# Weight blocks for the later slots fetched a turn ahead, in halves, with the cast behind the item's own

## The chip, the core and the metric

The kernel runs on one core of a Trainium2 chip. A core has five engines that run their own instruction rows in order and wait for each other by semaphores: TensorE (PE in the profile; PEld is its weight load), VectorE (DVE), ScalarE (ACT), GpSimd (POOL) and SyncE (SP), which here issues nearly all DMAs. The metric is the time of one execution on the device, in microseconds, as the median of several runs. One further execution is profiled; its own time is given beside the median.

## What is computed

A two-dimensional Fourier transform of x [8, 3072, 256] (real part), seen as 24576 tokens of 256 numbers, then a layer of 8 experts of which each token uses one, then a plain layer with a squared ReLU:

```python
X = np.fft.fft(np.fft.fft(x, axis=1), axis=2).real.astype(np.float32)
x = X.reshape(8 * 3072, 256)
e_idx = np.argmax(x @ w_gate, axis=1)            # the expert of a token
for e in range(8):
    mask = e_idx == e
    h = np.maximum(x[mask] @ w1[e], 0.0)         # w1[e] is 256 x 1024
    out[mask] = gate_w[mask, None] * eom[mask, e, None] * (h @ w2[e])   # w2[e] is 1024 x 256
h = np.maximum(out @ w_in, 0.0)                  # w_in is 256 x 2048
return (h * h) @ w_out                           # w_out is 2048 x 256
```

`gate_w` and `eom` are a softmax weight and a sigmoid of `x @ w_output_gate`. All is float32.

## The kernel before

A float32 matmul is made of three products of a rounded high part and a remainder: h is x cast to the type that PE reads (fp32r), l is x - h, and the product takes hh, hl and lh. So every operand is *split*: ACT casts, and DVE or POOL subtracts. In the names of the profile xh/xl, hh/hl, zh/zl, wih/wil and woh/wol are such pairs.

**Fourier part.** Eight batches go through `fft` and `group` (lines 148 to 343). DVE adds and multiplies along the first axis (tile X, lines 158 and 161), PE multiplies by tables loaded as trig (L258, SP) into pz, ACT casts zh (L273), DVE makes zl (L274), PE makes pd from them (L281). Tokens are sorted by expert and scattered by POOL into a DRAM array xs (L340), in groups of six scatters.

**Expert part.** Tokens are taken from xs in slots of 256, all of one expert (tile xr, L556). A slot has 12 items. Four a-items (`items_a`) do the expert layer: first matmuls into ph, then ACT casts hh (L682) and DVE makes hl (L683), then second matmuls into py. Eight c-items (`items_c`) do the last layer for the slot before: matmuls into ph, three ACT instructions (L853 rl, L854 square, L857 hh) and one of DVE (L858 hl) in `squares`, then matmuls into po, whose result goes out by POOL (L740). `push` gives the order: an item's first matmuls, its evacuation, and then the second matmuls of the item three before.

**Weights of a slot.** The first 40 slots ("single") hold the raw weights of their expert in two tiles r1 and r2 (`expert`, SP, L603 and L604), and split them on the way: ACT casts w (L615), POOL subtracts (L616). The later slots ("paired") read weights that were split beforehand from a DRAM array wq (L582, SP). `presplit` fills wq: for each of 64 blocks it fetches raw values (SP, L595), casts them into the first half of a tile cut (ACT, L596), subtracts into the second half (POOL, L597) and writes cut to wq (SP, L598). Raw and cut have one room each. It is a generator; `build` draws one block from it at every sixth item, from item 66 on.

**What sets the order.** `build` runs the items and draws from the Fourier generator at a set pace between them. The instruction order on each engine is then set by a scheduler that goes by data dependencies, rooms and program order; an instruction without an edge to the item next to which it was written can be moved far ahead. `issue_after(x)` puts the instructions in its block behind instruction x on their engine's row. In the order of before, the casts of presplit stand beside items 0 to 132 of 472 in the single stage.

Of the kernel before, what the change touches and what calls it, by code (L numbers as in the profile page):

```python
# [10 lines left out]
F32 = mybir.dt.float32  # L11
F32R = mybir.dt.float32r
# [3 lines left out]
AF = mybir.ActivationFunctionType  # L16
ALU = mybir.AluOpType
# [4 lines left out]
P = 128  # L22
S = 3072
D = 256
E = 8
# [74 lines left out]
class Kern:  # L100
# [485 lines left out]
    def presplit(self):  # L586

        nc = self.nc
        for e in range(E):
            for k in range(4):  # L590
                for j, src in enumerate((self.a["w1"][e].rearrange("(c p) f -> p c f", p=P)[:, :, k * 256:k * 256 + 256],
                                         self.a["w2"][e].rearrange("(c p) f -> p c f", p=P)[:, 2 * k:2 * k + 2])):
                    r = self.fp.tile([P, 2, 256], F32, name="raw")
                    o = self.fp.tile([P, 2, 2, 256], F32R, name="cut")
                    nc.sync.dma_start(out=r, in_=src)  # L595
                    nc.scalar.copy(out=o[:, 0], in_=r)  # L596
                    nc.gpsimd.tensor_tensor(out=o[:, 1], in0=r, in1=o[:, 0].bitcast(F32), op=ALU.subtract)  # L597
                    nc.sync.dma_start(out=self.wq[e, k, :, j * 1024:j * 1024 + 1024], in_=o.rearrange("p t c f -> p (t c f)").bitcast(F32))  # L598
                    yield

    def expert(self, q, w1, w2, **kw):
        flat = lambda w: w.rearrange("o (c p) f -> p (o c) f", p=P)
# [70 lines left out]
    def items_a(self, sl):  # L673
        st = {}
        for i in range(4):
            def mm1(i=i):
                st[i] = self.first(self.w[:, i, 0], self.w[:, i, 1], sl["x"], 0)

            def evac(i=i):
                h = self.ap.tile([P, 512], F32R, name="hh", bufs=4)  # L680
                l = self.ap.tile([P, 512], F32R, name="hl", bufs=4)
                self.nc.scalar.activation(out=h, in_=st[i], func=AF.Relu)  # L682
                self.evac = self.nc.vector.scalar_tensor_tensor(out=l, in0=st[i], scalar=0.0, in1=h.bitcast(F32), op0=ALU.max, op1=ALU.subtract)  # L683
                st[i] = (h, l)

            def mm2(i=i):
                if i == 0:
                    st["y"] = self.ps.tile([P, 512], F32, name="py", tag="y", bufs=1)
                h, l = st[i]
                for c in range(2):  # L690
                    k = slice(c * 256, c * 256 + 256)
                    for dc in range(2):
                        d = slice(dc * P, dc * P + P)
                        wh, wl = self.w[:, i, 2, c, d], self.w[:, i, 3, c, d]
                        self.products(st["y"][:, dc * 256:dc * 256 + 256], [(wh, h[:, k]), (wh, l[:, k]), (wl, h[:, k])],
                                      i == 0 and c == 0 and dc == 0, i == 3 and c == 1 and dc == 1)
                if i == 3:
                    if self.strassen:
                        ys = self.yp.tile([P, 2, SLOT], F32, name="ys", tag="yl" if sl["tail"] or self.both and sl["i"] % 2 else "yh", bufs=2)
                        self.nc.scalar.copy(out=ys, in_=st["y"].rearrange("p (c t) -> p c t", c=2))  # L700
                        if sl["tail"]:
                            self.nc.sync.dma_start(out=self.yt[:, :, bass.ds(sl["col"], SLOT)], in_=ys)
                        sl["y"] = ys
                    else:
                        sl["y"] = self.split(st["y"], self.yp, "y", 2)

            yield mm1, evac, mm2

    def items_c(self, sl):
# [140 lines left out]
    def squares(self, ps):  # L850

        r = self.yp.tile([P, 512], F32, name="rl", bufs=2)
        self.nc.scalar.activation(out=r, in_=ps, func=AF.Relu)  # L853
        self.nc.scalar.activation(out=ps, in_=r, func=AF.Square)  # L854
        h = self.ap.tile([P, 512], F32R, name="hh", bufs=4)
        l = self.ap.tile([P, 512], F32R, name="hl", bufs=4)
        self.nc.scalar.copy(out=h, in_=ps)  # L857
        self.evac = self.nc.vector.tensor_tensor(out=l, in0=ps, in1=h.bitcast(F32), op=ALU.subtract)  # L858
        return h, l

# [226 lines left out]
@with_exitstack  # L1087
def build(ctx, tc, a, B, plan, pace=1.25):

    kk = Kern(tc, a, B)  # L1090
    kk.n_tail = B * S // SLOT - sum(n for _, n in plan)
    nt = kk.n_tail + E - 1
    right = ctx.enter_context(ExitStack())
    left = ctx.enter_context(ExitStack())
    pool = lambda name, **kw: left.enter_context(tc.tile_pool(name=name, bufs=1, **kw))
    cp, wp, ps, dp = pool("cp"), pool("wp"), pool("ps", space=PSUM), pool("dp", space=DRAM)
    kk.ap = kk.tp = pool("ap")
    fp = right.enter_context(tc.tile_pool(name="fp", bufs=1, side="right"))
    kk.snaps = {nb: cp.tile([1, E], F32, name=f"snap{nb}") for nb, _ in plan}
    done = 0  # L1100

    def all_ffts():
        nonlocal done
        while done < B:
            yield from kk.fft(done)
            done += 1

    kk.fp = fp
    ffts = all_ffts()
    next(ffts)  # L1110
    with tc.tile_pool(name="st0", bufs=1) as st:
        kk.setup(cp, fp, st, ps, dp)
    kk.moe_setup(wp)

    def ffts_to(nb):
        while done < nb:
            next(ffts, None)

    tables = {}
    cut = kk.presplit()  # L1120

    def opener(w):
        def open_(u):
            nb, n = plan[w]
            if w not in tables:
                ffts_to(nb)
                with tc.high_priority():
                    if w < len(plan) - 1:
                        tab, ex = kk.table(n, kk.snaps[nb])
                        tables[w] = tab, kk.changes(ex), None  # L1130
                    else:
                        for _ in cut:
                            pass
                        right.close()
                        kk.tp = tp = right.enter_context(tc.tile_pool(name="tp", bufs=1, side="right", reuse_waits="tile"))
                        tab, ex = kk.table(n, kk.snaps[nb])
                        tab2, ex2 = kk.table(nt, kk.snaps[nb], tail=True)
                        tables[w] = tab, kk.changes(ex, ex2[:, 0:KEEP]), tab2
                        kk.zero_tails()
            tab, chg, tab2 = tables[w]  # L1140
            u["tab"] = tab2 if u["tail"] else tab
            u["chg"] = chg[:, u["i"]:u["i"] + 1]
        return open_

    units = []
    for w, (nb, n) in enumerate(plan):
        kinds = [False] * n
        if w == len(plan) - 1:
            kinds = [False, True, False] * KEEP + [False] * (n - 2 * KEEP)
        c = [0, 0]  # L1150
        for i, tail in enumerate(kinds):
            units.append(dict(i=i, j=c[tail], tail=tail, w=w, batches=nb, paired=w == len(plan) - 1, open=opener(w)))
            c[tail] += 1
    g = kk.run(units)
    ffts_to(plan[0][0])
    kk.yp = pool("yp")
    kk.early, kk.due, kk.rate = 12, 0.0, 1.25
    kk.other = (1, 2)
    kk.second = kk.second_weights()
    for _ in range(8):  # L1160
        next(g)

    acc, at = 0.0, 8
    ends = np.cumsum([12 * n for _, n in plan])
    for _ in g:
        at += 1
        if at > ends[0] and at % 6 == 0 and at < ends[2]:
            next(cut, None)
        w = int(np.searchsorted(ends, at, side="right"))
        if w + 1 < len(plan):  # L1170
            acc += pace * FFT_COST * (plan[w + 1][0] - plan[w][0]) / (12 * plan[w][1] - (8 if w == 0 else 0))
            while acc > 0:
                with tc.issue_after(kk.evac.ins) if at > ends[0] else ExitStack():
                    c, wait = next(ffts, (1e9, True))
                acc -= c
                if wait:
                    break
# [24 lines left out]
```

## Time and profile before

| quantity | value |
|---|---|
| median of 3 runs | 3777.5 us (3771.97 to 3778.32) |
| the profiled execution | 3795.63 us |
| its span in the trace | 3793.8 us |
| PE busy | 3578.2 us, 94% of the span |
| ACT, DVE, POOL busy | 57%, 56%, 28% |
| mean granted clock of PE | 0.981 of full speed |

The span is the profiled execution as its engines show it; the execution's own time is 1.8 us longer, and 18.1 us longer than the median. Single stage: to about 1767 us. The busy share is a mean over stages: below, the page's 40 slices (94.8 us each) show where it is lower, and tables by stretch give it in microseconds. "a <- b" in a list of waits reads: a stood still until b had come. L12 is a line of the kernel before.

### The profile page before, as it was taken

Reading aid. Unit: us, or ns where it says so; the run is one execution under the profiler, and the core shown is the slowest. Engines: PE = TensorE matmul, PEld = TensorE weight load, DVE = VectorE, ACT = ScalarE, POOL = GpSimd, SP = SyncE. Lnnn points to the kernel's source line nnn. Section 1 sums busy time; section 2 is a strip of 40 time slices with the busy share of each in tenths; the row PEclk is TensorE's granted clock in tenths of the full one; section 3 lists DMA queues with packets and bytes.
Section 4 is the critical chain, followed back from the end, with each engine's and each line's share of the span. In section 5 each row is a group of like instructions: output and inputs, shape, how many; then the busy total and the mean of one; then the engine's idle time right before and its main releaser. Section 6 shows DMA issues by size and latency. Waiting matters only on the chain. (4 is left out here: it accounts for less than half of the span.)

```text
span 3793.8 us, 76990 instructions
## 1 busy us (share of the span) xinstructions
PE 3578.2 (94%) x29484; PEld 3521.6 (93%) x29484; DVE 2118.2 (56%) x4043; ACT 2174.7 (57%) x4377; POOL 1047.9 (28%) x1196
## 2 busy tenths in 40 slices
PE   4578988999999999999999999999999999999998
PEld 4577888999999999999999999999899999999997
DVE  7975555576767576325344445444455555555554
ACT  3455555656666566666355555555566666656665
POOL 4765565445454455432000000000000000000000
PEclk8799999999999999999999999999999999999999
DMA  6445454322222211012234343443210100101000
GB/s 204 158 140 175 146 184 165 129 75 93 67 86 74 94 65 61 30 37 85 87 133 152 131 171 137 141 147 132 88 67 18 60 26 24 51 21 51 27 15 12
DMA packets 172851, 356.40 MB, mean 94 GB/s; under 512 B 21824, under 2 KB 125504, under 8 KB 157120
## 3 DMA queue, kind: packets, MB, share of 16 engines
q1 hardware_dynamic: 152960, 296.49, 23.4%
q0 software_dynamic: 19520, 54.94, 3.9%
q8 instruction: 235, 3.85, 0.4%
q14 instruction: 136, 1.11, 0.1%
HBM read 431.40 MB, written 89.85 MB: 137 GB/s over the span
## 5 line engine op out<-in xcount | busy, mean ns | idle before, releaser
L651 PE MATMUL po<-woh,hh 128*128 128x256 f32 x3072 | 861.7, 281 | 8.2 <-ACT hh L857 8.0
L651 PE MATMUL po<-wol,hh 128*128 128x256 f32 x3072 | 860.4, 281 | 3.0 <-POOL wol L414 3.0
L651 PE MATMUL po<-woh,hl 128*128 128x256 f32 x3072 | 859.5, 281 | 1.3 <-DVE hl L858 0.6
L651 PE MATMUL ph<-xh,w 128*128 128x256 f32 x3200 | 651.7, 285 | 27.9 <-DVE hl L683 15.4
L651 PE MATMUL py<-hh,w 128*128 128x256 f32 x3200 | 635.5, 282 | 1.0 <-ACT hh L682 0.6
L651 PEld LDWEIGHTS po<-woh,hh 128*128 128x128 f32 x3072 | 581.5, 189 | 12.4 <-ACT hh L857 11.9
L651 PEld LDWEIGHTS po<-wol,hh 128*128 128x128 f32 x3072 | 580.3, 189 | 3.4 <-POOL wol L414 3.4
L651 PEld LDWEIGHTS po<-woh,hl 128*128 128x128 f32 x3072 | 578.6, 189 | 5.2 <-DVE hl L858 4.5
L651 PEld LDWEIGHTS ph<-xh,w 128*128 128x128 f32 x3200 | 527.8, 191 | 29.4 <-DVE hl L683 15.8
L683 DVE SCALAR_TENSOR_TENSOR hl<-ph,hh 128x512 fp32r<-128x512 f32 x400 | 275.3, 689 | 481.9 <-ACT hh L682 466.2
L651 PEld LDWEIGHTS py<-hh,w 128*128 128x128 f32 x3200 | 519.8, 189 | 5.4 <-ACT hh L682 3.4
L682 ACT ACTIVATE hh<-ph 128x512 fp32r<-128x512 f32 x400 | 238.6, 597 | 483.0 <-PE ph L651 459.7
L616 POOL TENSOR_TENSOR w<-r,w 128x512 fp32r<-128x512 f32 x320 | 426.3, 1346 | 269.7 <-ACT w L615 268.3
L651 PE MATMUL ph<-xl,w 128*128 128x256 f32 x1600 | 456.1, 285 | 1.0 <-DVE xl L623 1.0
L651 PE MATMUL py<-hl,w 128*128 128x256 f32 x1600 | 453.4, 283 | 0.7 <-DVE hl L683 0.7
L858 DVE TENSOR_TENSOR hl<-ph,hh 128x512 fp32r<-128x512 f32 x320 | 220.0, 688 | 405.6 <-ACT hh L857 384.5
L740 POOL DMA_INDIRECT out<-ot,id x192 | 196.6, 1024 | 785.8 <-DVE ot L739 748.7
L651 PE MATMUL ph<-yh,wih 128*128 128x256 f32 x1280 | 372.7, 291 | 35.6 <-DVE hl L858 31.2
L645 POOL CAST id<-xr 128x2 uint32<-128x2 f32 x88 | 20.4, 232 | 1292.9 <-DMA xr<-xs 1286.1
L651 PE MATMUL ph<-yl,wih 128*128 128x256 f32 x1280 | 361.4, 282 | 1.0 <-issue 1.0
L651 PE MATMUL ph<-yh,wil 128*128 128x256 f32 x1280 | 361.6, 283 | 0.0
L858 DVE TENSOR_TENSOR hl<-px,hh 128x512 fp32r<-128x512 f32 x224 | 154.8, 691 | 325.2 <-ACT hh L857 323.5
(279 smaller groups left out, 8406.6 us busy)
## 6 DMA issues: line engine op xcount, KB each, us to landing
w<-wq SPq DMA_DIRECT2D x240, 1024.0 KB
r<-w SPq DMA_DIRECT2D x78, 1024.0 KB
wq<-cut SPq DMA_DIRECT2D x64, 512.0 KB
xr<-xs SPq DMA_DIRECT2D x100, 260.0 KB
raw<-w SPq DMA_DIRECT2D x64, 256.0 KB
trig<-c_trig SPq DMA_DIRECT2D x104, 128.0 KB
X<-x SPq DMA_DIRECT2D x8, 1024.0 KB
X<-x SPq DMA_DIRECT2D x8, 768.0 KB
```

The source lines that it names most:

```text
L616: nc.gpsimd.tensor_tensor(out=l, in0=r, in1=h.bitcast(F32), op=ALU.subtract)
L645: self.nc.gpsimd.tensor_copy(out=i, in_=ids)
L651: self.nc.tensor.matmul(out=out, lhsT=l, rhs=r, start=first and i == 0, stop=last and i == len(pairs) - 1, skip_group_check=True)
L682: self.nc.scalar.activation(out=h, in_=st[i], func=AF.Relu)
L683: self.evac = self.nc.vector.scalar_tensor_tensor(out=l, in0=st[i], scalar=0.0, in1=h.bitcast(F32), op0=ALU.max, op1=ALU.subtract)
L740: q = self.nc.gpsimd.indirect_dma_start(out=self.a["out"], out_offset=bass.IndirectOffsetOnAxis(ap=ids[:, t:t + 1], axis=0), in_=o[:, t, : ...
L858: self.evac = self.nc.vector.tensor_tensor(out=l, in0=ps, in1=h.bitcast(F32), op=ALU.subtract)
```

## The change

`presplit` works on 128 half units of [128, 256] instead of 64 blocks of [128, 512]. The raw tile has two rooms; the fetch for the next unit is given at the end of a unit's turn, the first one ahead of all. The tile cut is half as large and still has one room. The cast is placed, by `issue_after`, behind the last ACT instruction of the item that was written last (`self.cast`, L682 or L857 of before). `build` draws a unit at every third item, from item 75 on. In the changed file the lines of presplit are 594 (fetch), 602 (cast), 603 (subtract) and 605 (write); L615 becomes 623, L682 690, L853 to L858 become 861 to 866.

```diff
     def presplit(self):
 
         nc = self.nc
-        for e in range(E):
-            for k in range(4):
-                for j, src in enumerate((self.a["w1"][e].rearrange("(c p) f -> p c f", p=P)[:, :, k * 256:k * 256 + 256],
-                                         self.a["w2"][e].rearrange("(c p) f -> p c f", p=P)[:, 2 * k:2 * k + 2])):
-                    r = self.fp.tile([P, 2, 256], F32, name="raw")
-                    o = self.fp.tile([P, 2, 2, 256], F32R, name="cut")
-                    nc.sync.dma_start(out=r, in_=src)
-                    nc.scalar.copy(out=o[:, 0], in_=r)
-                    nc.gpsimd.tensor_tensor(out=o[:, 1], in0=r, in1=o[:, 0].bitcast(F32), op=ALU.subtract)
-                    nc.sync.dma_start(out=self.wq[e, k, :, j * 1024:j * 1024 + 1024], in_=o.rearrange("p t c f -> p (t c f)").bitcast(F32))
-                    yield
+        units = [(e, k, j, c) for e in range(E) for k in range(4) for j in range(2) for c in range(2)]
+
+        def fetch(e, k, j, c):
+            r = self.fp.tile([P, 256], F32, name="raw", bufs=2)
+            src = self.a["w2" if j else "w1"][e].rearrange("(c p) f -> p c f", p=P)
+            nc.sync.dma_start(out=r, in_=src[:, 2 * k + c] if j else src[:, c, k * 256:k * 256 + 256])
+            return r
+
+        r = fetch(*units[0])
+        yield
+        for (e, k, j, c), nxt in zip(units, units[1:] + [None]):
+            o = self.fp.tile([P, 2, 256], F32R, name="cut")
+            with self.tc.issue_after(self.cast.ins):
+                nc.scalar.copy(out=o[:, 0], in_=r)
+            nc.gpsimd.tensor_tensor(out=o[:, 1], in0=r, in1=o[:, 0].bitcast(F32), op=ALU.subtract)
+            to = self.wq[e, k, :, j * 1024:j * 1024 + 1024].rearrange("p (t c f) -> p t c f", t=2, c=2)
+            nc.sync.dma_start(out=to[:, :, c], in_=o.bitcast(F32))
+            r = nxt and fetch(*nxt)
+            yield
...
-                self.nc.scalar.activation(out=h, in_=st[i], func=AF.Relu)
+                self.cast = self.nc.scalar.activation(out=h, in_=st[i], func=AF.Relu)
...
-        self.nc.scalar.copy(out=h, in_=ps)
+        self.cast = self.nc.scalar.copy(out=h, in_=ps)
...
-        if at > ends[0] and at % 6 == 0 and at < ends[2]:
+        if at > ends[0] + 12 and at % 3 == 0 and at < ends[2]:
             next(cut, None)
```

ACT's row at the end of one slot's w casts, before. In the names, the number behind a tile is one use of it; r2_133 is the raw half of the expert's weights, py and ph are PE's results:

```order
L857 CAST hh_6073<-ph_6057 128x512
L622 CAST yh_6089<-py_5973 128x512
L615 CAST w_134<-r2_133 128x512
L596 CAST cut_18178<-raw_18177 128x512
L853 ACTIVATE rl_6111<-ph_6098 128x512
L854 ACTIVATE ph_6098<-rl_6111 128x512
```

The same place now:

```order
L865 CAST hh_6081<-ph_6065 128x512
L630 CAST yh_6097<-py_5975 128x512
L623 CAST w_134<-r2_133 128x512
L861 ACTIVATE rl_6119<-ph_6106 128x512
L862 ACTIVATE ph_6106<-rl_6119 128x512
L865 CAST hh_6122<-ph_6106 128x512
L602 CAST cut_6147<-raw_6025 128x256
```

The cast, ahead of the next item's evacuation before (L853 to L857), stands behind it now. Its block, number 18177 of the program before, was written for item 342 of the program; number 6025 was fetched beside this place.

SP's row around the same place, before:

```order
L598 DMA wq_135<-cut_17600 128x1024
L595 DMA raw_17834<-w2 128x2x256
...
L603 DMA r1_132<-w1 128x2x1024
L598 DMA wq_135<-cut_17835 128x1024
L595 DMA raw_18177<-w1 128x2x256
...
L604 DMA r2_133<-w2 128x8x256
```

And now:

```order
L605 DMA wq_135<-cut_6265 128x2x256
L594 DMA raw_6398<-w1 128x256
L605 DMA wq_135<-cut_6394 128x2x256
L594 DMA raw_6507<-w2 128x256
...
L611 DMA r1_132<-w1 128x2x1024
L605 DMA wq_135<-cut_6503 128x2x256
L594 DMA raw_6634<-w2 128x256
```

Before, a write of block n is followed by the fetch of block n + 1 (cut_17835 is made from raw_17834). Now the write of unit n is followed by the fetch of unit n + 2: cut_6394 is made from raw_6269, and raw_6398, fetched ahead of that write, becomes cut_6503.

## Rows read from the trace of the kernel before

**Rows 1.** The page's 40 slices (94.8 us each): busy tenths, and granted clock.

```profile
PE   4578988999999999999999999999999999999998
PEclk8799999999999999999999999999999999999999
```

**Rows 2.** By stretch: length, PE, PEld, DVE, ACT, POOL busy (instructions), clock, DMA share, GB/s.

```profile
220.00:700.00 480.00, 411.49 (x3231) 399.75 (x3230) 273.88 (x559) 263.15 (x546) 277.14 (x284) 0.94 0.50 165
700.00:1511.00 811.00, 794.14 (x6735) 786.05 (x6734) 539.22 (x1056) 500.56 (x1014) 405.89 (x449) 1.00 0.24 79
1511.00:1735.00 224.00, 222.93 (x1900) 222.89 (x1900) 71.06 (x124) 142.98 (x249) 83.32 (x80) 1.00 0.13 43
```

**Rows 3.** Waits, 220 to 705 us, ACT and PE: us in total, times, longest.

```profile
ACT cut L596 <- DMA raw<-w: 127.8, 46, 8.6
...
PE pd L281 <- ACT zh L273: 23.2, 15, 3.1
PE ph L651 <- DVE hl L858: 21.6, 12, 5.2
...
PE ph L651 <- DVE hl L683: 4.1, 2, 2.1
PE pt L631 <- DMA xr<-xs: 3.0, 1, 3.0
```

**Rows 4.** Waits, 705 to 1511 us, ACT and PE.

```profile
ACT rl L853 <- PE ph L651: 88.6, 105, 3.9
ACT w L615 <- PE ph L651: 87.1, 70, 2.0
...
PE ph L651 <- DVE hl L858: 5.1, 3, 2.6
PE pd L281 <- ACT zh L273: 4.4, 5, 1.3
```

**Rows 5.** In order of time, 300 to 312 us: start, length, instruction, [idle before].

```profile
303.38 0.43 SPq L595 DMA_DIRECT2D raw<-w  x1
...
307.18 0.62 ACT L596 CAST cut<-raw 128x512 fp32r<-128x512 f32 x1 [2.58 <-DMA raw<-w]
...
309.88 0.82 PE L281 MATMUL pd<-mh,zh 128*128 128x290 f32 x2 [3.05 <-ACT zh L273]
```

**Rows 6.** In order of time, 556 to 572 us, four engines.

```profile
563.12 0.38 SPq L595 DMA_DIRECT2D raw<-w  x1
...
567.23 0.62 ACT L596 CAST cut<-raw 128x512 fp32r<-128x512 f32 x1 [8.27 <-DMA raw<-w]
...
569.62 0.69 DVE L858 TENSOR_TENSOR hl<-ph,hh 128x512 fp32r<-128x512 f32 x1 [2.19 <-ACT hh L857]
...
570.37 0.58 PE L651 MATMUL ph<-yh,wih 128*128 128x256 f32 x1 [4.29 <-DVE hl L858]
```

**Rows 7.** By line: ns shortest/median/longest, first and last start in us, shapes.

```profile
L596 ACT CAST cut<-raw x64: 602/620/632, 32.3 to 694.6; 128x512 fp32r<-128x512 f32 x64
...
L597 POOL TENSOR_TENSOR cut<-raw,cut x64: 1261/1292/2251, 37.2 to 695.5; 128x512 fp32r<-128x512 f32 x64
...
L407 ACT CAST wih<-conv x16: 401/406/428, 66.2 to 140.7; 128x256 fp32r<-128x256 f32 x16
...
L413 POOL TENSOR_TENSOR conv<-conv,woh x16: 728/914/1717, 148.9 to 211.4; 128x256 f32<-128x256 f32 x16
...
L598 SPq DMA_DIRECT2D wq<-cut x64: 343/356/427, 38.5 to 696.8; - x64
...
L582 SPq DMA_DIRECT2D w<-wq x240: 73/220/370, 1783.1 to 3668.8; - x120
```

**Rows 8.** In order of time, ACT, 1635 to 1672 us: two a-items' w casts.

```profile
1665.94 0.62 ACT L615 CAST w<-r 128x512 fp32r<-128x512 f32 x1 [0.93 <-PE ph L651]
...
1668.79 0.62 ACT L615 CAST w<-r 128x512 fp32r<-128x512 f32 x1 [1.73 <-PE ph L651]
```

**Rows 9.** Groups by line, POOL, 705 to 1511 us: busy us, mean ns, idle before.

```profile
L340 POOL DMA_INDIRECT xs<-R,pi x108 | 118.5, 1097 | 79.3 <-DVE R L337 41.0 <-issue 25.7 <-ACT hh L857 5.2
```

## The prediction

> **What bounds the kernel now.** I read the slices of the page first, then the busy time by stretch, then the lists of waits, then two stalls in order of time. The slices show TensorE (PE) at nine tenths or more from the eighth slice on, and below that, at a lower granted clock, before it [rows 1]. So the first 700 us hold nearly all that is left to win. The stretches put a size on it [rows 2]. From 220 to 700 us PE is busy for 411.49 of 480 us and does 3231 matmuls, 6.73 a microsecond. From 700 to 1511 us the same mixture of Fourier work and expert items goes on, and PE does 6735 in 811 us, 8.30 a microsecond. At that pace the 3231 would take 3231 / 8.305 = 389 us, so the stretch holds **91 us** above what the next one shows to be possible. They are of two kinds. Idle time: 480 - 411.49 = 68.5 us, of which the later stretch's 16.9 us over 6735 matmuls (2.5 ns each) would leave 8; that is 60 us too much. Slow work: a matmul costs 411.49 / 3231 = 127.4 ns instead of 117.9, and 9.45 ns x 3231 = 30.5 us. The granted clock is 0.94 there and 1.00 later, and 6% of 411 us is 25 us. In the slices the clock is lowest where PE pauses most [rows 1], so a pause seems to cost more than its own length.
>
> What pauses it: in 220 to 705 us ScalarE (ACT) stands still for 127.8 us, 46 times, in front of the presplit's cast, because the raw block has not landed [rows 3]. PE does not read that cast's result at all. It waits for what stands behind it on ACT: for zh directly (23.2 us) and for hl, which VectorE makes from ACT's hh (21.6 and 4.1 us). In 705 to 1511 us, which holds no presplit cast (all 64 lie at 32.3 to 694.6 us, [rows 7]), the same waits are 4.4 and 5.1 us [rows 4]. Two stalls show the chain. At 303.38 us SP issues a raw fetch, the cast starts at 307.18 after 2.58 us of waiting, zh follows two instructions later, and PE has idled for 3.05 us at 309.88 [rows 5]. The second is worse: raw issued at 563.12, since one raw room forces it to wait for the subtract before it, cast at 567.23 after 8.27 us, hl at 569.62, PE at 570.37 after 4.29 us [rows 6]. The cast stands in ACT's row at a place where its data cannot yet be there.
>
> **The change part by part.** *Fetch one turn ahead, two rooms.* In the new order a write is followed by the fetch for the unit after the next, so a raw block is asked for two turns, six items, before its cast. An item in the calm stage takes 2.85 us (1665.94 to 1668.79, [rows 8]), so six are 17 us, against 3.8 us from issue to cast in [rows 5]. The wait of 127.8 us goes nearly whole. What PE gets of it: the lower bound is the waits that name the chain, 23.2 + 21.6 + 4.1 = 48.9 us, less what the later stretch would have of them (9.5 us x 485 / 806 = 5.7): 43 us. The upper bound is the 91. I take 43 + 25 of clock = **68 us**, because the low clock follows from the pauses, and leave the rest of the idle time (17 us) to VectorE's and the Fourier chain's own waits, which stay.
>
> *The cast placed behind the item's own, units half as large.* The casts leave ACT's first 500 us and spread over items 75 to about 460; the instructions that they now stand between ran at some 510 to 1735 us in the trace of before. Their number doubles. A cast of 128x512 takes 0.62 us, one of 128x256 0.406 [rows 7]: 64 x 0.62 = 39.7 us become 128 x 0.406 = 52.0 us. Where they come to, ACT is free for 811 - 500.56 = 310 us and 224 - 142.98 = 81 us [rows 2], and it waits for PE there, 88.6 and 87.1 us [rows 4], up to 1.73 us before one w cast [rows 8]. If every cast found a gap the cost is 0. If a cast delays PE whenever ACT is busy at its moment (62% of the time) it is 0.62 x 52 = 32 us. Since PE's waits of that stretch for ACT and VectorE come to under 10 us although ACT is 62% busy, PE has other work in hand there while ACT is late, and I take a quarter: **8 us**. This cover is the three items by which the second matmuls trail the first; if it is gone, the 32 us are due. A gain is excluded here, since nothing is taken from that stretch; what ACT saves in the early one is in the 68 us already.
>
> *Subtracts.* GpSimd's (POOL's) 64 of 1.29 us, 83 us, become 128 of some 0.91 us (the 128x256 row of [rows 7]), 117 us, at a place where POOL is busy for half of the time (405.89 of 811). PE waits for none of them. Queued behind them on POOL stand the splits of w and the scatters, and in front of them too: 0 in the sum, and the second rival below.
>
> *DMAs.* 128 on SP become 256, the same bytes. In the new order the r1 and r2 loads stand right behind a write whose subtract is next to the last split that frees their room, so SP reaches them about when the room comes free, as before. PE's longest wait for any DMA in the crowded stretch was one of 3.0 us [rows 3]. Taken at 0, at most 3 us.
>
> *The end of presplit.* The last write now comes near 1735 us instead of 697; the first read of wq was at 1783.1 [rows 7]. Both are set by the items around them and move together, so some 48 us stay between them. Cost 0; if the write came after the read's turn, the read would wait for what is missing.
>
> Sum: -68 + 8 = **-60 us**. The profiled execution took 3795.63 us, so 3735.6 in its terms; the median of the runs is 18.1 lower, and 3777.5 - 60 = 3717.5, rounded to **3718**.
>
> Here the Trainium skill speaks against the change. Its page "DMA: Bandwidth & Descriptors" (section "Bandwidth") wants transfers of 1 MiB or more, and the section "Anatomy of one DMA" gives each transfer a fixed part of about 2 us beside its bytes; it was fitted for another issue path than SP's. By it a 256 KB fetch takes an estimated 2.6 us and one of 128 KB 2.3, so halving saves 0.3 us of a wait and 128 more transfers buy 256 us of fixed parts. The trace has 3.8 us from issue to cast for 256 KB [rows 5]; by the page's fit the sum is unchanged while those parts lie beside other work, and it is the rival on the one cut room that asks whether they do.
>
> **The rivals.** *A, the forecast*: the pauses go, the pace of the later stretch nearly follows. For it: PE's waits name ACT, and the stretch without casts has the same work. Bounds: gain 91 and cost 0 give 3687, gain 43 and cost 8 give 3742.
>
> *B, the Fourier chain is next.* VectorE was busy for 273.88 of 480 us; in 389 us that is 70%, more than the 66% of the stretch behind (539.22 of 811). If its chain (oh, hl behind the long X instructions) then sets the pace, half of the 68 comes back: 3777.5 - 34 + 8 = 3751. For it: PE's waits in [rows 3] name hl as often as zh. Against: hl waits in turn for hh on ACT [rows 6].
>
> *C, one cut room, slower.* The room for the result is still one, so a cast must wait until the previous write has landed, on ACT, with rl, hh and zh queued behind it. The chain is cast 0.41, subtract 0.91, issue 0.36 or so, landing 3.8 at the fetch's price: 5.5 us of a turn of 3 x 2.85 = 8.55, which leaves 3 us. POOL is an in-order queue, and six scatters of 1.1 us [rows 9] in front of the subtract take 6.6 us. The mechanism decides if POOL's queue exceeds 3 us in most turns. Then the wait is 127.8 / 55 = 2.32 us a unit (55 of the casts lie in that stretch) for the 102 units ahead of 1511 us, 237 us on ACT, which at the exchange of before, 91 / 127.8 = 0.71, cost PE 168 us, against 91 won: 3777.5 + 77 = **3855**. Against it: scatters come in 18 bursts over 811 us (108 of them, [rows 9]), while the turns there number some 83 (102 of them from 510 to 1511 us, 9.8 us each), so most see no burst; and ACT's wait falls where ACT had time.
>
> *D, no change*: the idle time is PE's supply of Fourier work, and the stall moves to the next instruction of the same chain. Then 3777 within 8 us. Against: [rows 4] has no such wait at a higher pace.
>
> **How the numbers follow.** A 0.69, B 0.16, C 0.08, D 0.07. The time is A's: 3718. The range takes A's bounds and B, and D's upper part is left out with C: 3688 to 3768. A measurement here tells a difference of 0.2%, 7.6 us, from none. Faster by more: A and B less 0.01, 0.84. Within: D and that 0.01, 0.08. Slower: C, 0.08.
>
> **What would show it.** Right: the wait of ACT at the cast for its raw block falls from 127.8 to under 10 us; the matmuls of the first 700 us are done some 55 to 70 us sooner, with a granted clock near 0.98 there; the casts show at 0.41 us; the pace between there and the end of the single stage stays at 8.2 to 8.3 a microsecond. Wrong by C: ACT waits at the cast for a DMA named wq, over 100 us in all, and PE's waits for zh and hl spread over the whole cast stretch. By B: the casts wait for nothing, and PE's idle time in the early stretch is still over 40 us, put down to VectorE. By D: the same idle time with other names.

## The result and the profile after

The kernel after takes **3694.7 us** (median of 4, 3691.24 to 3696.61), the kernel before 3777.8 in the same measurement: a ratio of 0.9783, 95% interval 0.9766 to 0.9799, or 83 us less. The forecast was 3718, with a range of 3688 to 3768, so the direction and the range hold, and the gain is 83 us where the sum said 60.

The slices of after are the same view as [rows 1], now 92.4 us each. PE is at nine tenths from the third slice on and not from the eighth; the granted clock reads nine tenths or more from the third slice on in both:

```profile
PE   4599999999999999999999999999999999999998
PEclk9799999999999999999999999999999999999999
```

ACT's waits at the presplit's cast over the whole run (where from, us, times, longest), beside the 127.8 us of [rows 3]:

```profile
ACT cut L602 <- DMA wq<-cut: 41.4, 15, 6.5
ACT cut L602 <- DMA raw<-w: 3.5, 1, 3.5
```

The wait for the raw block is all but gone. A third of its size has come back as a wait for the write of the one cut room, at another place: all 128 casts now lie between 423 and 1673 us. By line, as in [rows 7]:

```profile
L602 ACT CAST cut<-raw x128: 393/408/412, 423.0 to 1673.0; 128x256 fp32r<-128x256 f32 x128
L603 POOL TENSOR_TENSOR cut<-raw,cut x128: 723/743/1786, 423.9 to 1673.4; 128x256 fp32r<-128x256 f32 x128
L605 SPq DMA_DIRECT2D wq<-cut x128: 382/384/860, 424.6 to 1674.2; - x128
```

ACT in order of time shows what a cast looks like when it meets its block. It starts behind hh without a wait, and the instruction behind it still waits for PE, not PE for it:

```profile
541.57 0.62 ACT L623 CAST w<-r 128x512 fp32r<-128x512 f32 x1 [0.94 <-PE ph L659]
542.09 0.59 ACT L690 ACTIVATE hh<-ph 128x512 fp32r<-128x512 f32 x1
542.58 0.40 ACT L602 CAST cut<-raw 128x256 fp32r<-128x256 f32 x1
543.90 0.27 ACT L283 COPY R<-pd 128x129 f32<-128x129 f32 x1 [0.92 <-PE pd L281]
```

**Where the time came from.** The profiled execution of before took 18.1 us more than its median, that of after only 1.9 more. So the kernel before was profiled a second time (run b2, below: 3774.25 us, near the median), and the comparison is made with that one. Times at equal *items* are compared, not equal times: an item is counted by its hh on ACT, and the stages are item 12 to 130 (where all but seven of the casts of before lay), 130 to 460 (the rest of the single stage), and the paired slots behind. By stretch (length, then busy us and instructions of PE, PEld, DVE, ACT, POOL, clock, DMA share, GB/s), the first two stages in the second profile of before:

```profile
188.60:694.00 505.40, 433.45 (x3358) 421.70 (x3357) 300.56 (x600) 276.35 (x575) 297.46 (x302) 0.92 0.49 160
694.00:1756.20 1062.20, 1051.42 (x8957) 1045.48 (x8956) 640.72 (x1289) 672.78 (x1306) 501.92 (x544) 1.00 0.22 71
```

The same two stages of after:

```profile
181.10:599.50 418.40, 399.04 (x3314) 392.09 (x3313) 290.14 (x601) 257.24 (x535) 250.02 (x262) 0.98 0.32 104
599.50:1676.90 1077.40, 1060.68 (x8995) 1054.56 (x8994) 641.52 (x1204) 703.53 (x1416) 597.21 (x653) 1.00 0.34 109
```

The first stage is 505.4 - 418.4 = **87 us** shorter. PE's idle time there went from 72.0 to 19.4 us, 53 of the 87, and its busy time for nearly the same matmuls from 433.5 to 399.0, 34 of them, with the granted clock up from 0.92 to 0.98. Ahead of item 12 after is 7.5 us earlier (181.1 against 188.6). The second stage, to which most of the casts moved, is **15 us** longer, 6 in idle time and 9 in busy time. The paired slots take 2 us more. Together 87 + 7.5 - 15 - 2 = 77.5, which is the difference of these two executions, 3774.25 - 3696.61 = 77.6. Stages cut by items do not hold quite the same matmuls: after has 44 fewer in the first and 38 more in the second. At some 0.12 us each that is about 5 us, so at equal matmuls I estimate 82 us gained in the first stage and 11 lost in the second; of the 34 us of busy time, 29 are then slower matmuls (129.1 ns each against 120.4).

PE's waits in the first stage, second profile of before and then after:

```profile
PE ph L651 <- DVE hl L858: 22.5, 10, 6.1
PE pp L308 <- DVE oh L302: 21.2, 7, 6.7
PE pd L281 <- ACT zh L273: 15.7, 11, 3.0
```

```profile
PE ph L659 <- DVE hl L866: 7.7, 3, 5.9
PE ph L659 <- DVE hl L691: 4.0, 2, 2.2
...
PE pp L308 <- DVE oh L302: 0.3, 1, 0.3
```

The wait for zh is no longer in the list, and the one for oh, which looked like VectorE's own, has gone with it. The longest stall for oh shows why: VectorE's copy LG, five instructions ahead of oh, waits for ACT's copies R, and ACT had stood at the cast (second profile of before):

```profile
333.70 0.62 ACT L596 CAST cut<-raw 128x512 fp32r<-128x512 f32 x1 [6.23 <-DMA raw<-w]
334.90 0.19 DVE L286 COPY LG<-pd 128x32 f32<-128x32 f32 x1 [6.70 <-ACT R L284]
336.89 0.21 DVE L302 TENSOR_TENSOR oh<-small,ix 128x48 bf16<-128x48 f32 x1
337.15 0.20 PE L308 MATMUL pp<-oh,trib 128*128 128x48 bf16 x1 [6.70 <-DVE oh L302]
```

ACT had stood at a cast for its raw block in the same way ahead of each of the five stalls for oh over 1 us in that stage.

### The profile page after: what moved, and what is told of

Its sections match the earlier page's. It is cut to its first block, busy times and chain, and to the rows that moved or that the text cites. A ratio compares the mean times of both kernels' runs of the same rounds, so it can differ in the third digit from the quotient of the medians.

```text
span 3694.9 us, 77339 instructions
## 1 busy us (share of the span) xinstructions
PE 3546.9 (96%) x29484; PEld 3500.7 (95%) x29484; DVE 2118.7 (57%) x4043; ACT 2189.9 (59%) x4441; POOL 1089.0 (29%) x1260
```

## The experiments

Eleven runs. The two theories at first: **P** (place), that a cast must stand behind its item's own work, and **F** (fetch), that two rooms and the fetch one turn ahead bring the gain. A third, **S** (spacing), came up on the way.

**e1: the placement alone.** The kernel before, whole blocks, one raw room, every sixth item, with

```diff
-                    nc.scalar.copy(out=o[:, 0], in_=r)
+                    with self.tc.issue_after(self.cast.ins):
+                        nc.scalar.copy(out=o[:, 0], in_=r)
```

and `self.cast` set as in after.

> The kernel before with one change: the presplit's cast is placed behind the last ACT instruction of the item beside which it was written. Whole blocks of 128x512, one raw room, one cut room, every sixth item from item 66 as before. Theory P (place): what cost time was a cast standing ahead of other work at a place where its block could not yet be there; the place alone brings the gain, since a turn of six items (17 us) covers the fetch. It expects 3690 to 3710 us, under 15 us of ACT waits for the raw block, and PE some 92 us ahead of the kernel before at about item 190. Theory F (fetch): two rooms and the fetch one turn ahead bring it; it expects 3765 to 3785 us here, with ACT still waiting some 100 us at the cast for its raw block.

Measured: 3696.7 us, ratio 0.9794 (0.9773 to 0.9815), the same as after. ACT does not wait at the cast at all; the only row on it is POOL's wait for it:

```profile
L597 ACT CAST cut<-raw x64: 608/616/627, 387.3 to 1634.1; 128x512 fp32r<-128x512 f32 x64
...
  POOL cut L598: 30.0, 21
```

One edit of the three (placement, two rooms with the early fetch, halves at every third item) does it. F falls.

**e2: everything but the placement.** The kernel after, with

```diff
-            with self.tc.issue_after(self.cast.ins):
-                nc.scalar.copy(out=o[:, 0], in_=r)
+            nc.scalar.copy(out=o[:, 0], in_=r)
```

> The kernel after without the placement: half units, two raw rooms, the fetch one turn ahead, every third item from item 75, but nothing holds the cast behind the item's own, and in the order the casts go back to the first items. Theory P: the gain goes. The casts then run as fast as rooms and DMAs let them, 128 turns with two transfers each, ACT waits over 120 us in all at the cast, for the raw block or for the cut room's write, and the time is 3770 to 3830 us. Theory F: 3690 to 3720 us, as after, with under 20 us of such waits.

Measured: 3795.6 us, ratio 1.0058 (1.0038 to 1.0079): slower than before. The casts have gone back to the front of ACT's row, 128 of them from 28.8 to 860.6 us, 1.36 items apart, and wait for the write:

```profile
L601 ACT CAST cut<-raw x128: 388/406/451, 28.8 to 860.6; 128x256 fp32r<-128x256 f32 x128
...
  DMA wq<-cut: 192.8, 80
...
  DMA raw<-w: 14.1, 3
```

Without the placement, two raw rooms and the early fetch only move the wait from the raw block to the cut room. Two rooms of each kind without the placement were not tried.

**e3: one raw room.** The kernel after with `bufs=1` for raw.

> The kernel after with one raw room instead of two; halves, places and turns as after, so that a block is fetched one turn (8.5 us) ahead of its cast and not two. Theory P: 3690 to 3700 us, no difference from after that can be told, ACT's waits at the cast for the raw block up to 20 us in all. Theory F: 3720 us or more, over 60 us of waits for the raw block.

Measured: 3697.3 us, ratio 0.9798 (0.9778 to 0.9818); after itself was at 0.9783 and, in a later measurement, 0.9795. No difference can be told, though the waits were larger than P had expected:

```profile
ACT cut L602 <- DMA raw<-w: 49.6, 18, 7.4
```

**e4 and e10: two cut rooms.** The kernel after with

```diff
-            o = self.fp.tile([P, 2, 256], F32R, name="cut")
+            o = self.fp.tile([P, 2, 256], F32R, name="cut", bufs=2)
```

> The kernel after with two rooms for cut, so that a cast no longer waits for the landing of the write before it; ACT waited 41.4 us for that in the profile of after, 15 times. If ACT's waits there still cost PE (the slower rival of the prediction in small, at the exchange of 0.71 us of PE per us of ACT), the time falls by up to 29 us, to 3666 us. If they lie where ACT has time, as the prediction took it, it is 3685 to 3697 us, under 0.2% from after, though those waits go to under 5 us.

Measured: 3688.9 us, ratio 0.9776 (0.9755 to 0.9797); not to be told from after. So it was run again with five rounds beside after on one chip.

> The kernel after, unchanged, to stand beside the next run on one chip: 3691 to 3698 us.

> The kernel after with two rooms for cut, again, with more rounds. Its lead over after grew by 9 us in the first profiles, at the places of after where ACT had waited 41.4 us for the write of cut. If those waits cost PE, it is 4 to 10 us faster than after on the same chip, 3684 to 3692 us; if the first difference was chance, within 3 us of it.

Measured: after 3695.3 us (3694.0 to 3699.7; ratio 0.9795, 0.9782 to 0.9808), with two cut rooms 3685.0 us (3681.2 to 3687.2; 0.9765, 0.9752 to 0.9779). The ranges of the runs are apart: **10 us less than after**, and 88 less than before. ACT no longer waits for a DMA at the cast (one wait of 2.7 us, for GpSimd, is left), and the item stages are 413.2 and 1072.7 us:

```profile
176.80:590.00 413.20, 396.44 (x3317) 389.43 (x3316) 288.00 (x601) 257.66 (x535) 246.00 (x262) 0.99 0.32 105
590.00:1662.70 1072.70, 1058.59 (x8995) 1052.69 (x8994) 648.12 (x1204) 705.33 (x1416) 602.88 (x652) 1.00 0.34 109
```

**b2: the kernel before, profiled again.**

> The kernel before, unchanged, for a second profile. The profiled execution of before took 18.1 us more than the median of its runs, and the profiled execution of after only 1.9 more, so the two traces differ by 99 us where the medians differ by 83. If the 18 us belong to that one execution, this profile takes 3770 to 3783 us and shows in which stretch they lay. If every profiled execution of this kernel bears them, it takes 3790 to 3800 us. Either way ACT's waits at the presplit's cast for raw should be 110 to 135 us.

Measured: 3774.25 us, so the 18 us belonged to the first profiled execution. It had lost 4 us before item 12 and 15 between items 130 and 460 (1077.0 us there against 1062.2), and 4 in the paired slots; the stage with the casts is alike, 504.0 and 505.4. ACT's wait for raw is there again: 142.0 us in the whole run, 137.1 in the first item stage:

```profile
ACT cut L596 <- DMA raw<-w: 137.1, 43, 9.6
```

**e6: no split at all.** In the kernel before the raw values go straight from w1 and w2 into both halves of wq; cast and subtract are left out:

```diff
-                    r = self.fp.tile([P, 2, 256], F32, name="raw")
...
-                    nc.gpsimd.tensor_tensor(out=o[:, 1], in0=r, in1=o[:, 0].bitcast(F32), op=ALU.subtract)
...
+                    for t in range(2):
+                        nc.sync.dma_start(out=self.wq[e, k, :, j * 1024 + t * 512:j * 1024 + t * 512 + 512].rearrange("p (c f) -> p c f", c=2), in_=src)
```

> The kernel before with the presplit's cast and subtract left out: the raw values go from w1 and w2 straight into both halves of wq, two transfers a block, so the paired slots compute with weights that were not split. It tells what presplit costs on ACT, POOL and SBUF in all. Theory P: after pays almost nothing for its 128 casts and subtracts in the later place, so this is within 12 us of after, 3680 to 3700 us. If the 128 casts and subtracts still cost the 8 us of the prediction's sum or more, it is 3660 to 3680 us. If the early stretch was held by the DMAs of presplit and not by its cast, it stays near before, 3750 us or more.

Measured: 3684.1 us, ratio 0.9761 (0.9745 to 0.9778). So cast and subtract, with the waits at them, cost before some 93 us (3776.7 - 3684.1) and cost after 11. The transfers are still there: all 128 are given out by 278 us, and the DMA share between items 12 and 130 is 0.45, against 0.49 in before and 0.32 in after. The stage takes 414.8 us all the same, so it was not held by presplit's DMAs. From item 130 to 460 e6 needs 1063.5 us, as the second profile of before does, which has no presplit there:

```profile
184.20:599.00 414.80, 397.08 (x3307) 389.92 (x3306) 293.40 (x597) 252.22 (x515) 228.85 (x244) 0.99 0.45 139
599.00:1662.50 1063.50, 1056.77 (x9002) 1051.73 (x9001) 641.37 (x1291) 673.76 (x1307) 504.97 (x544) 1.00 0.22 70
```

**e7: a unit at every item.** The kernel after without `at % 3 == 0`, to shorten a turn below the chain of one unit.

> The kernel after with a unit at every item instead of every third, so 128 units beside items 73 to 200 and none behind. A turn is then one item, 2.9 to 3.4 us, while cast, subtract, issue and landing of the one cut room take some 5 us. If a cast behind the item's own costs nothing whatever it waits, the time is 3690 to 3710 us. If the slower rival of the prediction is right about the point from which it decides (the chain longer than a turn), every item of that stretch is stretched to the chain: about 2 us x 128 = 256 us more on ACT, of which ACT's free time takes a part; 3800 to 3950 us, with over 200 us of ACT waits at the cast for the write of cut.

Measured: 3801.3 us, ratio 1.0071 (1.0051 to 1.0091): slower than before, though every cast stands behind its item's own. Waits at the cast, items 73 to 226:

```profile
ACT cut L602 <- DMA wq<-cut: 186.8, 86, 8.2
```

So P in its plain form falls: a placed cast that waits is not free. Against e6 the run loses 117 us with 187 us of waits, 0.63 us of PE for each.

**e8: the placement with the spacing of before.** In the kernel before the casts stood 2.06 items apart on ACT. Run e1 with every second item instead of every sixth:

```diff
-        if at > ends[0] and at % 6 == 0 and at < ends[2]:
+        if at > ends[0] and at % 2 == 0 and at < ends[2]:
```

> The kernel of the run with the placement alone (whole blocks, one raw room, cast behind the item's own), with a block at every second item instead of every sixth: 64 blocks beside items 66 to 196. In the kernel before the casts stood 2.06 items apart on ACT without being placed, so this keeps its spacing and changes the place only. Theory P (place): a cast behind the item's own costs little whatever its spacing; 3695 to 3715 us. Theory S (spacing): the chain of one block, cast 0.62, subtract 1.29, two issues 0.75, landing 3.8, is 6.5 us and with POOL's queue longer than two items, so ACT waits again, 100 to 150 us, and at the 0.65 us of PE per us of ACT that the run with a unit at every item showed the gain of 77 us mostly goes: 3750 to 3790 us.

Measured: 3761.2 us, ratio 0.9968 (0.9957 to 0.9980). Nearly all of the gain is gone, and the wait of before is back, as large, with each cast behind its item's own:

```profile
ACT cut L597 <- DMA raw<-w: 144.5, 49, 10.5
```

S holds: what decides is how far apart the casts stand, against what one block's chain takes (cast, subtract, write issue, fetch issue, landing). In time the casts stand 19.8 us apart on average in e1, 9.8 in after and 7.9 in e8, its waits included; the expectation of e8 put the chain of a whole block at an estimated 6.5 us and more. The casts of e8 lie at items 62 to 188, so it is not the early stretch as such that makes them costly. Where inside an item a cast stands was not varied at the wide spacing. The placement matters because it holds the casts to the spacing in which they were written; without it the scheduler pulls them together at the front. Over the runs, with what each takes above e6:

| run | items between casts | ACT waits at the cast for a DMA, us | time above e6, us |
|---|---|---|---|
| e1, whole blocks | 6 | 0 | 13 |
| e10, halves, two cut rooms | 3 | 0 | 1 |
| after | 3 | 45 | 11 |
| e3, one raw room | 3 | 50 | 13 |
| before | 2.06 | 142 (b2) | 93 |
| e8, whole blocks | 2 | 145 | 77 |
| e2, not placed | 1.36 | 207 | 112 |
| e7 | 1.2 | 187 | 117 |

From after to e10, 45 us of waits go and 10 us of time, a quarter. Where a wait comes at most turns, the time above e6 is half to two thirds of the waits. e1 pays 13 us with no wait, so the last column is not all waits; its casts and subtracts are longer (0.616 and 1.297 us against 0.408 and 0.743), but that these are the reason was not tried.

**e11: the subtract on VectorE.** The version with two cut rooms and `nc.vector` in the place of `nc.gpsimd` in presplit.

> The kernel after with two rooms for cut and the presplit's subtract on VectorE instead of GpSimd. With two rooms no cast waits for a DMA any more, and items 130 to 460 still took 1072.7 us against 1063.5 without cast and subtract. If the 9 us come from the 128 subtracts on GpSimd (they stand in its row ahead of splits and scatters, and VectorE's long X instructions run longer while GpSimd computes: 90 us above their shortest there instead of 70), the time falls by 3 to 9 us from the version with two rooms, to 3676 to 3683 us. If any engine pays alike for 128 more instructions beside PE's suppliers (VectorE at about 0.42 us each, 54 us), it is 3683 to 3693 us.

Measured: 3684.6 us, ratio 0.9766 (0.9752 to 0.9780), the same as e10; items 130 to 460 take 1070.5 us instead of 1072.7. The 7 to 9 us that this stage takes above e6 do not come from the subtracts' standing on GpSimd. Whether the casts, the subtracts on any engine, the transfers or a single execution's chance make them stays open.

The best version is that of e10, 3685.0 us, with e11 beside it. It lies 1 us above e6, so little is left to win from cast and subtract as they stand. That is a balance: e10 is 9 us slower than e6 behind item 130, and reaches item 12 earlier (176.8 us; the same kernel in e4 181.1, e6 184.2), in the stretch in which e6 gives out its transfers. What the transfers cost no run shows.

## Why the prediction came out as it did

- *The bound.* Right: the idle time and the slow clock of the first 700 us came from ACT standing in front of the cast. The two kinds were sized at 60 and 30 us and measured 53 and 34, or an estimated 29 at equal matmuls. The ceiling of 91 was set by a pace that was itself low: the first execution's later stretch did 8.30 matmuls a microsecond, the second's 8957 / 1062.2 = 8.43 in about the same items. Two readings were off without harm: zh is the fifth instruction behind the cast of [rows 5] and not the second, and [rows 1] has the clock below nine tenths in the first two slices alone, lowest in the second, where PE is not at its least. That the pauses brought the lower clock rests on the 0.94 of [rows 2]; with the pauses gone the stage has 0.98.
- *The 68 us for the waits.* The step that was too small. "I take 43 + 25 of clock" left 17 us to "VectorE's and the Fourier chain's own waits, which stay". They did not: the wait for oh fell from 21.2 to 0.3 us, since VectorE was late for the same reason. The list of [rows 3] had that wait too, with 13.5 us between the rows shown (line below), and the sum took nothing for it. The stage gave 87, an estimated 82 at equal matmuls. The nine casts ahead of 220 us were taken at nothing; before item 12 after is 7.5 us ahead. Whether casts or transfers held that start is not told apart: e6, with the transfers and no casts, reaches item 12 at 184.2 us, between the two.

```profile
PE pp L308 <- DVE oh L302: 13.5, 6, 4.4
```

- *The 8 us for the casts' new place.* 15 us between the two profiles, an estimated 11 at equal matmuls, 14 against e6 in the same stage. Of these the second cut room takes 5 away (1077.4 to 1072.7), and 10 in the whole run (e10): waits that the sum took at zero, as part of the rival. The 9 that stay above e6 are near the 8, but what makes them is open.
- *Two rooms, halves.* Costed as what makes the wait go. They are not needed: e1 does it with one room and whole blocks, e3 with one room. In so far the forecast had luck: the edit that it credited with the end of the wait was not the one that ended it.
- *Subtracts and DMAs.* A half subtract took 0.743 us, not 0.91. On the number of transfers the Trainium skill ("DMA: Bandwidth & Descriptors", section "Bandwidth") had spoken against halves; e1 with 64 whole blocks and e3 with 128 halves, both with one room, take 3696.7 and 3697.3 us. No cost of the smaller transfers shows here, where they lie beside other work.
- *The end of presplit.* The last write came at 1674.2 us and the first read of wq at 1690.5: 16 us apart and not 48. The last unit hides still, with a third of the cover.
- *Rival B* fell with the wait for oh: no bound by VectorE shows. *Rival C* had its mechanism right and its condition not met. Its wait came to 41 us and not 237, on 15 of 128 casts. The longest of them, 6.5 us, was made as the rival said, with six scatters (L340) on GpSimd from 765.11 us between the cast before it and that cast's subtract (lines below). Where the condition was forced (e7), its price was right: 0.63 us of PE for each of ACT where 0.71 was used, and slower than before. *Rival D* fell.

```profile
762.71 0.41 ACT L602 CAST cut<-raw 128x256 fp32r<-128x256 f32 x1
773.70 0.98 POOL L340 DMA_INDIRECT xs<-R,pi  x1 [0.31 <-issue]
774.69 0.75 POOL L603 TENSOR_TENSOR cut<-raw,cut 128x256 fp32r<-128x256 f32 x1
775.46 0.39 SPq L605 DMA_DIRECT2D wq<-cut  x1
777.75 0.41 ACT L602 CAST cut<-raw 128x256 fp32r<-128x256 f32 x1 [6.54 <-DMA wq<-cut]
```

- *The signs named.* Raw wait under 10 us: 3.5. Clock near 0.98: 0.98. Casts at 0.41 us: 0.408. Early matmuls 55 to 70 us sooner: 94 at item 130, with the 7.5 from the start, or an estimated 89 at equal matmuls. Pace behind at 8.2 to 8.3: 8995 / 1077.4 = 8.35.

The reason itself was half right. The prediction blamed the place of a cast, ahead of other work. It is the turn against the chain: a cast between two evacuations is behind the one and ahead of the other wherever it stands, and e8 waits as before did with each one placed.

## What to carry to other kernels

For a background stream with few rooms, compare the time between two of its steps with the whole chain that frees a room and fills it again, and hold the steps to that spacing in the instruction order; the scheduler here, where it saw no edge, pulled them together, and a second raw room then only moved the wait. When a long wait on one engine goes, waits of its neighbours that look like their own can go with it. Here the ceiling from the next stretch (91 us) was a better size for the stage than the waits that name the engine with the clock's share (68). And one profiled execution that lies well above the median should be taken again before its paces are used.

## What the hardware showed besides

Two executions of the same program differed by 15 us in a stage of 1062 us, spread over it, with the granted clock at 1.00 in both; why stays open.

VectorE's additions of X run long while GpSimd computes. DVE and then POOL in order of time, the kernel before:

```profile
559.08 8.35 DVE L161 TENSOR_TENSOR X<-X 128x1016 f32<-128x1016 f32 x1
```

```profile
558.85 2.57 POOL L616 TENSOR_TENSOR w<-r,w 128x512 fp32r<-128x512 f32 x2
561.34 1.32 POOL L597 TENSOR_TENSOR cut<-raw,cut 128x512 fp32r<-128x512 f32 x1
562.59 3.77 POOL L616 TENSOR_TENSOR w<-r,w 128x512 fp32r<-128x512 f32 x3
```

The addition, 1.2 us at the median of its line and of its shape, took 8.35 us, and ended 1 us after the sixth subtract of GpSimd in a row. All 17 instructions on X over 3 us in that run (L158 and L161) overlap two or more of GpSimd's subtracts. The Trainium skill ("SBUF — State Buffer", section "Terms") has VectorE and GpSimd share a pair of ports by an exclusive lock, held for an instruction; the trace agrees in that the addition ends only when GpSimd's row has, here after six instructions and not one. For presplit it did not matter: with the subtracts on VectorE (e11) the time is the same.
